# Value products of 33 groups as three float16 passes in an attention and MLP block

## The chip, the cores and the metric

One core of one Trainium2 chip runs the whole program. The metric is device time in microseconds (us), the median of the runs shown; less is better. Engines are named as the profile names them: PE is TensorE, PEld its weight loads, DVE is VectorE, ACT is ScalarE, POOL is GpSimd, SP is SyncE, which issues most of the transfers.

## The reference

Sequence 2048, width 512, 32 heads of 16 dimensions, an MLP of width 1792; all inputs and the output are float32.

```python
def _A_ref(x, wqkv, wo):
    q, k, v = ...            # (x @ wqkv), 32 heads of 16
    scores = jnp.einsum("bhqd,bhkd->bhqk", q, k) * Dh ** -0.5
    p = _softmax(scores, axis=-1)
    o = jnp.einsum("bhqk,bhkd->bhqd", p, v)
    return o.transpose(...).reshape(B, S, D) @ wo

def _B_ref(x, w1, w2):
    return silu(x @ w1) @ w2

h = x + _A_ref(_layernorm(x), A_wqkv, A_wo)
h2 = h + _B_ref(_layernorm(h), B_w1, B_w2)
```

## The kernel before

Float32 products are made from float16 parts: a number is split into a high half h and a rest l, and a product is three float16 matmuls (h·h, l·h, h·l). The one product that stays float32 is that of the softmax weights with the values.

The work of the attention is cut into 32 *items*: four heads times one of four blocks of 512 query rows; items 0 to 7 belong to the first block, 8 to 15 to the second and so on. An item has 16 chunks c of 128 keys. One item and one chunk make a *group* g = 16·i + c; there are 512. The loop over g (L1461) runs one *step* per group:

- four score matmuls (`scores`, L495), keys as weights, queries moving, 64 rows deep, so that two of different array halves run side by side. Rows 48 and 49 of a query tile hold the row's maximum, which the product so subtracts;
- four exponentials on ACT (`weigh`, L504; recorded at the helper's L113), from PSUM into a tile `pt` of 128 x 512 float32. There are 14 such buffers;
- up to four *maxima* for later items (`one_max`, L426): a 48-row matmul and a reduction on DVE (L307);
- two steps later (LAG), the *value products* of a group (`values`, L893): four float32 matmuls, one per head, with 17 columns of `va` (16 values and a one, whose product is the softmax's sum) as weights and `pt` moving. The four outputs lie at partitions 0, 32, 64 and 96 of one bank `pv`, that is, in four column tiles. The profile counts each as two matmuls, so a block has eight records;
- over 112 steps each from the fifth step of items 9, 17 and 25 on, the MLP of the query block before, as *chains*: 14 chains of 12 first products (`first_of`, L1148) and then 4 chains of 42 second products (`second_of`, L1154; three a step, so 14 steps each), cut in two halves of 64 rows and laid beside the score and maximum matmuls (`beside_products`, L1243; `half_product`, L1192). At the end of a chain of first products ACT scales the sum and SiLU is made on ACT and POOL (`bend`, L1165); at the end of a second chain (`end_second`) ACT scales (the tile `g`) and, one step later, POOL adds it to the rows `ot` and SP stores them.

After chunk 15 of an item `finish_item` (L911) copies `pv` to `pvs` on ACT, sends the sums to memory, and puts the division on an agenda at given numbers of steps after: `sums` fetches them (2), `invert` (L980) makes 1/x by four small POOL operations (6), `spread` copies the result over partitions by DMA (8), `divide` multiplies on POOL (10, odd items only).

All orders are written out: `mm`, `act`, `pool`, `dve` and `dma` pin each instruction to its place on its engine, and each engine executes in that order. Key and query tiles `ks`, `qs` form a ring of five (RING); an item's slot is i % 5. The lines of the profile are those of the helpers: L99 matmul, L106 POOL, L113 ACT, L123 DVE, L129 SP.

Of the kernel before, what the change touches and what calls it, by code (L numbers as in the profile page):

```python
# [20 lines left out]
P = 128  # L21
# [17 lines left out]
LN = 2.0 ** 10  # L39

BOUND = 23.0
PIECES = 14, 14, 4
# [5 lines left out]

LAG = 2
PTS = 14  # L50

RING = 5

HEADS = [(0, 1), (0, 0), (1, 1), (1, 0)]
# [37 lines left out]
def attention_mlp_kernel(ctx: ExitStack, tc: tile.TileContext, x, wqkv, wo, w1, w2, out):  # L92
# [100 lines left out]
    nc.gpsimd.memset(minus, -1.0)  # L193
    ones = const.tile([P, P], F32, name="ones")
    nc.gpsimd.memset(ones, 1.0)
    powers = const.tile([P, 4], F32, name="powers")
    both_s, both_w = powers[:, :2], powers[:, 2:]
    qk_s, qk_w, v_w = (powers[:, n:n + 1] for n in (0, 2, 3))
    qk_e, qk_0, v_f = (const.tile([P, 1], F32, name=name) for name in ("qk_e", "qk_0", "v_f"))

    factors = const.tile([P, 15], F32, name="factors")
    sigma, inverse = factors[:, :4], factors[:, 4:8]
    w1_s, w2_s, wo_s, o_s = (sigma[:, n:n + 1] for n in range(4))
# [47 lines left out]
    va = vpool.tile([P, KC, H, DH + 1], F32, name="va")  # L251

    def rows_of_head(t, h):
        return t[h * DH:(h + 1) * DH].rearrange("d s n -> (d s) n")

    def load_k(i, k, lo=0, n=S):
        a, j = HEADS[k]
        h = 4 * (i % 8) + 2 * a + j
        dma(ks[i % RING][64 * j:64 * j + 48, a, lo:lo + n], rows_of_head(kd, h)[:, lo:lo + n])

    def load_q(i, k):
        a, j = HEADS[k]
        h = 4 * (i % 8) + 2 * a + j
        lo = i // 8 * 512
        dma(qs[i % RING][64 * j:64 * j + 48, a, :], rows_of_head(qd, h)[:, lo:lo + 512])

# [24 lines left out]
    def maximum(i, kb, qt, a, j, n):  # L291

        piece = piece_of(i, a)
        width = 1 if i == LAST else 2
        if piece not in mx:
            mx[piece] = small.tile([P, 64], F32, name="mx", bufs=RING + 1)[:, :32 * width].rearrange(
                "p (j a q k) -> p j a q k", j=2, a=width, k=4)
            left[piece] = 32 * width
        heads = (0, 1) if j is None else (j,)
        for m, h in enumerate(heads):  # L300
            mm(space[:, n + m, :], qs[i % RING][64 * h:64 * h + 48, a, qt * P:qt * P + P],
               ks[i % RING][64 * h:64 * h + 48, a, kb * 512:kb * 512 + 512], start=True, stop=True)
        of = mx[piece][:, :, a % width, qt, kb]
        if j is None:
            pin(nc.vector.tensor_reduce(of, space[:, n:n + 2, :], axis=AX.X, op=ALU.max))  # L305
        else:
            pin(nc.vector.tensor_reduce(of[:, j:j + 1], space[:, n, :], axis=AX.X, op=ALU.max))  # L307
# [42 lines left out]
    def place_far(piece):  # L350

        i, a = piece
        n = 16 if a is None else 8
        mt = small.tile([P, P], F16, name="mt", bufs=1)
        pin(nc.sync.dma_start(mt, wide.pop(piece), transpose=True))
        split.pop(piece)

        def out():
            for j in range(2):
                rows = qs[i % RING][64 * j + 48:64 * j + 50, slice(None) if a is None else slice(a, a + 1)]  # L360
                dma(rows.rearrange("r a n -> r (a n)").rearrange("r (a b) -> r a b", b=P), mt[n * j:n * j + n, :])
            placed.add(piece)

        if at["attention"]:
            soon(1, out)
        else:
            out()

    def place_max(piece):
# [9 lines left out]
        def out():  # L379
            for j in range(2):  # L380
                dst = qs[i % RING][64 * j + 48:64 * j + 50, slice(None) if a is None else slice(a, a + 1)]
# [108 lines left out]


    def pt_tile(name):
        return bp.tile([P, 512], F32, tag="pt", name=name, bufs=PTS)

    def scores(g, k, kind="st"):  # L495

        i = g // KC
        a, j, c = head(g, k)
        assert piece_of(i, a) in placed
        ps = bank(kind)  # L500
        mm(ps, ks[i % RING][64 * j:64 * j + 64, a, c * P:(c + 1) * P], qs[i % RING][64 * j:64 * j + 64, a, :],
           start=True, stop=True)
# [39 lines left out]

    rest_sq = const.tile([P, sum(PIECES)], F32, name="rest_sq")
    norms = const.tile([P, 4], F32, name="norms")
# [24 lines left out]
    def set_factors():  # L569
# [4 lines left out]
        for to, a, f in ((h_f, inverse[:, :1], 1 / LN), (g_s, w1_s, 1 / 32.0), (g_half, w1_s, 1 / 64.0),  # L574
                         (out_f, inverse[:, :1], 32.0), (o_minus, o_s, -1.0), (o_twice, o_s, 2.0)):
            pool("tensor_scalar", to, a, f, None, op0=ALU.mult)
        pool("tensor_tensor", out_f, out_f, inverse[:, 1:2], ALU.mult)
        pool("tensor_tensor", wo_f, inverse[:, 2:3], inverse[:, 3:], ALU.mult)
# [27 lines left out]
    def measure(meanwhile):  # L606
# [58 lines left out]
    def project_v(b, t):  # L665
# [105 lines left out]
    for b in range(NB):  # L771
# [7 lines left out]
        for n, (kind, k) in enumerate(units + vs if b else units):  # L779
# [131 lines left out]
    def finish_item(i):  # L911
# [28 lines left out]
    def finish_part():  # L940
        pvs = bp.tile([P, 512], F32, name="pvs", bufs=1)
        dve("tensor_copy", pvs, pv)
        o_t = zp.tile([P, 4, P], F32, name="o_t", tag="oh")
        pool("memset", o_t, 0.0)
# [4 lines left out]
    def divide_part(part, pvs, o_t, kind="st"):  # L949
# [3 lines left out]
        halves = ps.rearrange("p t (m j r) -> p t m j r", m=2, r=32)[:, :, :, :, :DH + 1]  # L953
        both = gp.tile([P, 4, 2, DH + 1], F32, name="both", bufs=1)
# [4 lines left out]
        dve("tensor_scalar", rc, rc, o_s, None, op0=ALU.mult)  # L959
        to = o_t[:, :, 64 + 32 * part:96 + 32 * part].rearrange("p t (j d) -> p t j d", j=2)  # L960
# [104 lines left out]
    def load_rows(b, t):  # L1065
# [3 lines left out]
        else:  # L1069
            hx[t] = ks[(LAST + 1) % RING].rearrange("p a n -> p (a n)").bitcast(F32)[:, t * D:(t + 1) * D]  # L1070
        dma(hx[t], x[n * P:(n + 1) * P, :])
# [89 lines left out]
    def end_first(f, ps):  # L1161
# [3 lines left out]
        def bend():  # L1165
            t = zp.tile([P, 512], F32, name="t", tag="oh")
            act("activation", t, z, AF.Tanh, scale=0.5)
# [262 lines left out]
    def maxima(g):  # L1430

        i, c = divmod(g, KC)
        ready = at["ready"] = min(ITEMS, i + RING - (0 if c == KC - 1 else 1)) * 64
        late_now = at["step"] in late
# [26 lines left out]
    for g in range(groups):  # L1461
# [5 lines left out]
        if (g in beside) != (g - 1 in beside):  # L1467
# [37 lines left out]
        if g == 1:  # L1505
            dve("memset", pv, 0.0)
        at["group"] = g
        n = maxima(g)
# [75 lines left out]
```

## Time and profile before

| | us |
|---|---|
| median of 3 runs | 1544.13 (1543.99 to 1544.88) |
| the profiled execution, its own time | 1544.18 |
| its span | 1542.3 |
| PE busy | 1531.9 (99%) |
| DVE busy | 1364.3 (88%) |
| ACT busy | 1240.0 (80%) |
| POOL busy | 575.1 (37%) |

The time is that of the whole execution, the span goes from the first to the last instruction; the two lie 1.9 us apart. Busy times of the engines overlap, so shares alone don't say what bounds a stage. The table of stretches gives busy times for a window of the span; the timeline gives each instruction's start and length, with the idle time ahead of it and what ended that in brackets; a count behind an x means that many records in a row. A row with `xN | a, b | c` has N instructions, a us busy in all, b ns each, and c us of idle time ahead of them.

### The profile page before, as it was taken

What the parts mean: (1) busy time and instruction counts of PE and PEld (TensorE: products, weight loads), DVE (VectorE), ACT (ScalarE), POOL (GpSimd) and SP (SyncE); (2) the same over time, 40 slices, a digit from 0 to 9 for tenths busy, and PEclk for the clock granted to TensorE, in tenths of its full rate; (3) what the DMA queues carried; (4) which work ended last, traced back from release to release, by engine and by line L of the source; (5) the groups of instructions that cost most, each with busy time, mean ns of one, the idle gap of its engine ahead of it and who ended that gap; (6) DMA issues with size and microseconds to landing.
All of it is one profiled execution on the core that took longest, in us unless ns stands there. A gap on an engine that the chain in (4) does not pass through costs nothing.

```text
span 1542.3 us, 30754 instructions
## 1 busy us (share of the span) xinstructions
PE 1531.9 (99%) x11408; PEld 494.6 (32%) x11408; DVE 1364.3 (88%) x2168; ACT 1240.0 (80%) x2410; POOL 575.1 (37%) x782
## 2 busy tenths in 40 slices
PE   9999999999999999999999999999999999999999
PEld 6433322222222333333322333333322333332354
DVE  7899999999999999999999999999999999994322
ACT  5555699999987899888888998888878889888632
POOL 6643453544544444411144444301153444212100
PEclk9999999999999999999999999999999999999999
DMA  6667423333434122245424112444433221335332
GB/s 220 167 170 237 135 80 93 119 96 109 111 89 103 35 63 63 82 147 152 144 64 103 43 46 62 123 131 129 140 81 92 57 56 43 103 103 168 111 91 74
DMA packets 137058, 163.32 MB, mean 106 GB/s; under 512 B 44112, under 2 KB 81040, under 8 KB 136908
## 3 DMA queue, kind: packets, MB, share of 16 engines
q1 hardware_dynamic: 132156, 152.85, 34.6%
q10 hardware_dynamic: 4752, 8.52, 2.1%
q8 instruction: 89, 1.46, 0.4%
q14 instruction: 61, 0.50, 0.1%
HBM read 126.48 MB, written 24.63 MB: 98 GB/s over the span
## 4 chain that ended last, share of the span: by engine, by line
PE 93%; DVE 3%; ACT 2%; issue 1%; POOL 0%; DMA 0%; SPq 0%; POOLq 0%; ACTq 0%
PE ps L99 93%; ACT pt L113 1%; DVE mx L305 1%; DVE mx L307 1%; PE ps L102 1%; DMA ks<-in_A_x_dram 0%; DVE pvs L123 0%; POOL wv_l L106 0%; DVE ks L123 0%; DVE st L123 0%; ACT pvs L113 0%; ACT g L113 0%; DVE ot L123 0%; DVE xtl L123 0%; POOL rs L106 0%
## 5 line engine op out<-in xcount | busy, mean ns | idle before, releaser
L307 DVE TENSOR_REDUCE mx<-ps 128x1 f32<-128x512 f32 x1842 | 1146.1, 682 | 56.2 <-PE ps L99 12.0
L113 ACT ACTIVATE pt<-ps 128x512 f32<-128x512 f32 x2048 | 1049.7, 606 | 130.8 <-PE ps L99 128.7
L99 PE MATMUL ps<-ks,qs 48*128 48x512 f16 x2048 | 666.9, 380 | 2.6 <-DVE mx L307 1.5
L99 PE MATMUL ps<-qs,ks 64*128 64x512 f16 x2048 | 624.8, 377 | 0.6
L99 PE MATMUL ps<-pt,va 128*17 128x512 f32 x4096 | 539.1, 598 | 0.6
L99 PE MATMUL ps<-hts,w 64*128 64x512 f16 (+2 forms) x1212 | 285.0, 372 | 0.0
L99 PEld LDWEIGHTS <-ks 64*128 64x128 f16 x2048 | 174.0, 94 | 223.8 <-issue 177.6
L99 PE MATMUL ps<-w,gates 64*128 64x512 f16 (+1 forms) x938 | 230.3, 378 | 0.2 <-ACT g L113 0.2
L99 PEld LDWEIGHTS <-qs 48*128 48x128 f16 x2048 | 166.4, 94 | 67.7 <-issue 28.4
L99 PEld LDWEIGHTS <-w 64*128 64x128 f16 (+1 forms) x1212 | 101.6, 95 | 236.9 <-ACT pt L113 107.2
L106 POOL TENSOR_TENSOR ri<-rc,minus 128x16 f32<-128x16 f32 x31 | 90.6, 2924 | 208.8 <-DMA rc<-dn 208.8
L99 PEld LDWEIGHTS <-gates 64*128 64x128 f16 (+1 forms) x1082 | 88.7, 95 | 222.5 <-ACT pt L113 97.8
L99 PEld LDWEIGHTS ps<-pt,va 128*17 128x17 f32 x4096 | 68.1, 95 | 195.3 <-issue 186.6
L305 DVE TENSOR_REDUCE mx<-ps 128x2 f32<-128x1024 f32 x103 | 119.1, 1218 | 4.3 <-PE ps L99 3.5
L113 ACT ACTIVATE g<-ps,factors 128x512 f32<-128x512 f32 x80 | 54.7, 684 | 65.1 <-PE ps L99 61.0
L106 POOL TENSOR_SCALAR t<-t,factors 128x512 f32<-128x512 f32 x42 | 29.0, 691 | 184.0 <-ACT t L113 184.0
L113 ACT ACTIVATE ks<-ps 128x512 f32<-128x512 f32 x30 | 17.9, 597 | 51.9 <-PE ps L99 46.6
L106 POOL TENSOR_TENSOR ot<-ot,g 128x512 f32<-128x512 f32 x12 | 15.3, 1271 | 111.6 <-ACT g L113 111.6
L123 DVE SCALAR_TENSOR_TENSOR gh<-g,factors,gh 128x512 f16<-128x512 f32 x14 | 10.5, 752 | 52.1 <-ACT gh L113 52.1
L106 POOL TENSOR_TENSOR t<-t,g 128x512 f32<-128x512 f32 x42 | 53.7, 1279 | 3.5
L106 POOL TENSOR_TENSOR sl<-ks,sh 128x512 f16<-128x512 f32 x30 | 34.7, 1156 | 50.4 <-ACT sh L113 36.9
L106 POOL TENSOR_SCALAR nm<-nm 128x16 f32<-128x16 f32 (+1 forms) x42 | 10.8, 256 | 107.1 <-DVE nm L321 105.5
(158 smaller groups left out, 1029.7 us busy)
## 6 DMA issues: line engine op xcount, KB each, us to landing
w<-w2d SPq DMA_DIRECT2D x182, 256.0 KB
ks<-kd SPq DMA_DIRECT2D x120, 192.0 KB
w<-w1d SPq DMA_DIRECT2D x56, 256.0 KB
ks<-in_B_w_dram ACTq DMA_DIRECT2D x28, 256.0 KB
w<-in_B_w_dram SPq DMA_DIRECT2D x28, 256.0 KB
qs<-qd SPq DMA_DIRECT2D x128, 48.0 KB
kd<-sh SPq DMA_DIRECT2D x16, 256.0 KB
qd<-sh SPq DMA_DIRECT2D x16, 256.0 KB
```

The lines of the kernel that those rows point to most:

```text
L99: return tc.keep_in_program_order(nc.tensor.matmul(*a, **k))
L102: tc.keep_in_program_order(nc.tensor.transpose(*a))
L106: tc.keep_in_program_order(getattr(nc.gpsimd, op)(*a, **k))
L113: ins = getattr(nc.scalar, fn)(*a, **k)
L123: pin(getattr(nc.vector, fn)(*a, **k))
L305: pin(nc.vector.tensor_reduce(of, space[:, n:n + 2, :], axis=AX.X, op=ALU.max))
L307: pin(nc.vector.tensor_reduce(of[:, j:j + 1], space[:, n, :], axis=AX.X, op=ALU.max))
```

## The change

In 33 groups the exponentials' results are split into float16 halves, and the value products are three float16 passes in place of one float32 product. A group is one of them (`in_halves`) where its chunk is 3, 7, 11 or 15, its item is 10 to 30, and the steps from one before it to three after it lie among the second products; these are groups 207, 211, ... 255, then 335 to 383, and 463 to 487.

- ACT writes the exponential into a tile `raw` (float32, three buffers). The high half h is a cast of it, on POOL for two of the four heads (k < 2) and otherwise on ACT, except in steps with c = 2 and those that end a chain, where all are on POOL. The rest l is a subtraction on POOL. h and l lie in the two halves of the `pt` tile.
- `values` issues for such a group twelve matmuls with weights of their own: v_h·h for the four heads, then v_l·h, then v_h·l.
- The halves of the four chunks of `va` are made in item 10 by POOL (`split_chunk`) into the fifth pair of key and query tiles; from then on the ring has four slots (`slot`, `loaded`), and loads are issued one item later.
- The constant rows `fix_q` of the query tiles, zero so far, raise all exponents by a constant; `measure` computes it by three small POOL operations. The scale of the values, so far part of `v_f` and undone by `o_s`, is a constant, and the first four chunks of `va` are multiplied once more on POOL, in the projection of the third block.
- The steps of the division are 2, 7, 9, 11 in place of 2, 6, 8, 10. Buffers for maxima are four in place of six.

The core of the diff:

```diff
+START = 2
+HALVED = 3, 7, 11, 15
...
+FEWER = 2 * RING
...
-    nc.gpsimd.memset(fix_q, 0.0)
+    nc.gpsimd.memset(fix_q, 1.0)
+    raised = const.tile([16, 1], F32, name="raised")
...
+    def slot(i):
+        return i % RING if i < FEWER else (i - FEWER) % (RING - 1)
+
+    def loaded(i):
+
+        return min(ITEMS, i + RING if i < FEWER else max(FEWER + RING - 1, i + RING - 1))
...
+    def halves_of(t):
+        return t.bitcast(F16)[:, :512], t.bitcast(F16)[:, 512:]
+
+    width = H * (DH + 1)
+    spare_k, spare_q = (t.rearrange("p a n -> p (a n)") for t in (ks[RING - 1], qs[RING - 1]))
+    parts = [spare_k[:, n * width:(n + 1) * width] for n in range(7)] + [spare_q[:, :width]]
+    split_v = [(parts[n], parts[4 + n]) for n in range(4)]
...
+    def in_second(g):
+
+        return (g - marks[0]) % (8 * KC) - BEHIND - 4 * FC
+
+    def in_halves(g):
+
+        i, c = divmod(g, KC)
+        return FEWER <= i < LAST and c in HALVED and all(in_second(x) in range(START, 4 * FC) for x in (g - 1, g + 3)) and g < KC * LAST - 8
+
+    def split_chunk(n):
+
+        (h, l), v = split_v[n], va[:, HALVED[n]].rearrange("p h d -> p (h d)")
+        pool("tensor_copy", h, v)
+        low(l, v, h, "pool")
...
             pts[g, k] = pt_tile("pt")
+            if in_halves(g):
+                raw, (h, l) = zp.tile([P, 512], F32, name="raw", tag="oh", bufs=3), halves_of(pts[g, k])
+                ins = act("activation", raw, ps, AF.Exp, scale=qk_f)
+                if k < 2 or at["next"] % KC == 2 or in_second(at["next"]) % FC == FC - 1:
+                    pool("tensor_copy", h, raw)
+                else:
+                    act("copy", h, raw)
+                low(l, raw, h, "pool")
+                return ins
             return act("activation", pts[g, k], ps, AF.Exp, scale=qk_f)
...
-        dve("reciprocal", v_f, v_w)
-        pool("tensor_scalar", v_f, v_f, 1 / LN, None, op0=ALU.mult)
         dve("reciprocal", qk_e, qk_s)
         dve("scalar_tensor_tensor", qk_e, qk_e, SCALE, qk_e, op0=ALU.mult, op1=ALU.mult)
+        pool("tensor_scalar", raised, qk_s[:16], qk_s[:16], RAISE * math.log(2) / (14 * MX * SCALE), op0=ALU.mult, op1=ALU.mult)
+        pool("tensor_scalar", raised, raised, MOST, None, op0=ALU.min)
+        pool("tensor_scalar", fix_q, fix_q, raised, 1.0, op0=ALU.mult, op1=ALU.mult)
...
-        act("mul", va[:, 4 * b + t, :, 0:DH], ps.rearrange("p (h d) -> p h d", d=DH), v_f)
+        act("mul", va[:, 4 * b + t, :, 0:DH], ps.rearrange("p (h d) -> p h d", d=DH), 1 / (16.0 * LN))
...
+            if b == 2 and 2 <= n:
+                pool("tensor_scalar", va[:, n - 2, :, 0:DH], va[:, n - 2, :, 0:DH], v_s, 1.0, op0=ALU.mult, op1=ALU.mult)
...
     def values(g):
         i, c = divmod(g, KC)
         n = KC if i < LAST else HALF
+        if in_halves(g):
+            h_l, v_l = [halves_of(pts.pop((g, k))) for k in range(4)], split_v[HALVED.index(c)]
+            for m, (x, v) in enumerate(((0, 0), (0, 1), (1, 0))):
+                for k in range(4):
+                    a, j, keys = head(g, k)
+                    h = 4 * (i % 8) + 2 * a + j
+                    mm(pv[32 * k:32 * k + DH + 1, :], v_l[v][:, (DH + 1) * h:(DH + 1) * (h + 1)], h_l[k][x],
+                       start=False, stop=m == 2 and c == KC - 1)
+            if c == KC - 1:
+                finish_item(i)
+            return
...
-        steps = (1, 3, 4, 6) if u == 7 else (2, 6, 8, 10)
+        steps = (1, 3, 4, 6) if u == 7 else (2, 7, 9, 11)
         for n, fn in zip(steps, (sums, invert, spread, divide) if u % 2 else (sums, invert, spread)):
             soon(n, fn, i)
         if i == ITEMS - 2:
-            soon(10, divide_half)
-            soon(12, split_half)
+            soon(11, divide_half)
+            soon(13, split_half)
...
-        if i + RING - 1 < ITEMS and 6 <= c < 14:
-            (load_k if c % 2 else load_q)(i + RING - 1, c // 2 - 3)
+        if loaded(i) > loaded(i - 1) and 6 <= c < 14:
+            (load_k if c % 2 else load_q)(loaded(i) - 1, c // 2 - 3)
...
+        if i == FEWER and c % 3 == 2 and c < 12:
+            split_chunk(c // 3)
```

On PE the order is the same but for the blocks. This is the block of group 207, the first of the 33: before, one row for four float32 matmuls (each loads its weights by itself), between the last score matmul and the next step's second products (`gates` holds the hidden rows as weights, `w` moves).

```order
L99 LDWEIGHTS qs_107
L99 MATMUL ps<-ks_106,qs_107 128x512
L99 LDWEIGHTS ks_104
L99 MATMUL ps<-qs_105,ks_104 128x512
L99 MATMUL ps<-pt,va 17x512 x4
L99 LDWEIGHTS gates
L99 MATMUL ps<-w,gates 128x512
```

And in the changed kernel, the block's first pass and the beginning of its second; `ks4_104` and `qs4_105` are the fifth key and query tiles, which now hold halves of the values.

```order
L109 MATMUL ps_66<-qs3_103,ks3_102 128x512
L109 LDWEIGHTS ks4_104
L109 MATMUL ps_66<-pt_7871,ks4_104 17x512
L109 LDWEIGHTS ks4_104
L109 MATMUL ps_66<-pt_7907,ks4_104 17x512
L109 LDWEIGHTS ks4_104
L109 MATMUL ps_66<-pt_7879,ks4_104 17x512
L109 LDWEIGHTS ks4_104
L109 MATMUL ps_66<-pt_7915,ks4_104 17x512
L109 LDWEIGHTS qs4_105
L109 MATMUL ps_66<-pt_7871,qs4_105 17x512
```

Four matmuls have become twelve, each with a weight load of its own, at the same place. The second and third pass take the same four `pt` tiles in the same order, the third with `ks4_104` as weights again.

On ACT, around the copy of item 12's sums (`pvs`); before, exponentials alone stand on both sides of it:

```order
L113 ACTIVATE t<-g 128x512
L113 ACTIVATE pt<-ps 128x512 x20
L113 COPY pvs<-ps 128x512
L113 ACTIVATE pt<-ps 128x512 x30
L113 ACTIVATE g<-ps,factors 128x512
```

In the changed kernel, the same stretch; `raw` is written by exponentials, and a cast of it follows where it is ACT's.

```order
L123 ACTIVATE pt<-ps 128x512 x6
L123 ACTIVATE raw<-ps 128x512 x2
L123 CAST pt<-raw 128x512
L123 ACTIVATE pt<-ps 128x512 x2
L123 ACTIVATE raw<-ps 128x512 x2
L123 CAST pt<-raw 128x512
L123 ACTIVATE pt<-ps 128x512 x8
L123 COPY pvs<-ps 128x512
L123 ACTIVATE pt<-ps 128x512 x2
L123 ACTIVATE raw<-ps 128x512 x2
L123 ACTIVATE pt<-ps 128x512 x2
```

Each of the two casts ahead of the copy stands behind the last exponential of its step; group 211 behind the copy has none in its first step (c = 2), where POOL casts.

On POOL, around the division of item 12, which stands in item 13; `ri`, `rc` are the inversion, `ot<-ot,g` the add of an MLP chain, `nm` and `ns` the maxima's split. Before:

```order
L106 TENSOR_TENSOR gates<-t,gates 128x512
L106 TENSOR_TENSOR ri<-rc,minus 128x16
L106 TENSOR_TENSOR rc<-rc,ri 128x16
L106 TENSOR_SCALAR rc<-rc,factors 128x16
L106 TENSOR_TENSOR ri<-ri,rc 128x16
L106 TENSOR_TENSOR ot_1868<-ot_1868,g 128x512
L106 TENSOR_SCALAR nm<-nm 128x16
```

In the changed kernel, from group 215 (chunk 7 of item 13) to group 219 (chunk 11):

```order
L116 CAST pt<-raw 128x512
L116 TENSOR_TENSOR pt<-raw,pt 128x512 x2
L116 TENSOR_TENSOR ri<-rc,minus 128x16
L116 TENSOR_TENSOR rc<-rc,ri 128x16
L116 TENSOR_SCALAR rc<-rc,factors 128x16
L116 TENSOR_TENSOR ri<-ri,rc 128x16
L116 TENSOR_TENSOR ot_1873<-ot_1873,g 128x512
L116 CAST pt<-raw 128x512
L116 TENSOR_TENSOR pt<-raw,pt 128x512 x2
L116 CAST pt<-raw 128x512
L116 TENSOR_TENSOR pt<-raw,pt 128x512
L116 TENSOR_SCALAR nm<-nm 128x16
```

The inversion and the add now stand between the pieces of two halved groups, ahead of the second one's first cast.

More of the change, by code (lines that the diff above doesn't have):

```diff
@@ L39 @@
 LN = 2.0 ** 10
+RAISE = 14
+MOST = 2.0 ** 15
 BOUND = 23.0
@@ L193, in attention_mlp_kernel @@
     nc.gpsimd.memset(minus, -1.0)
-    ones = const.tile([P, P], F32, name="ones")
-    nc.gpsimd.memset(ones, 1.0)
     powers = const.tile([P, 4], F32, name="powers")
-    both_s, both_w = powers[:, :2], powers[:, 2:]
+    both_s, both_w, v_s = powers[:, :2], powers[:, 2:], powers[:, 1:2]
     qk_s, qk_w, v_w = (powers[:, n:n + 1] for n in (0, 2, 3))
-    qk_e, qk_0, v_f = (const.tile([P, 1], F32, name=name) for name in ("qk_e", "qk_0", "v_f"))
+    qk_e, qk_0 = (const.tile([P, 1], F32, name=name) for name in ("qk_e", "qk_0"))
     factors = const.tile([P, 15], F32, name="factors")
     sigma, inverse = factors[:, :4], factors[:, 4:8]
-    w1_s, w2_s, wo_s, o_s = (sigma[:, n:n + 1] for n in range(4))
+    w1_s, w2_s, wo_s = (sigma[:, n:n + 1] for n in range(3))
     h_f, g_s, out_f, wo_f, o_minus, o_twice, g_half = (factors[:, n:n + 1] for n in range(8, 15))
     fix_q = const.tile([16, 512], F16, name="fix_q")
-    nc.gpsimd.memset(fix_q, 0.0)
+    nc.gpsimd.memset(fix_q, 1.0)
+    raised = const.tile([16, 1], F32, name="raised")
     fix_k = const.tile([16, 512], F16, name="fix_k")
@@ L258, in load_k @@
         h = 4 * (i % 8) + 2 * a + j
-        dma(ks[i % RING][64 * j:64 * j + 48, a, lo:lo + n], rows_of_head(kd, h)[:, lo:lo + n])
+        dma(ks[slot(i)][64 * j:64 * j + 48, a, lo:lo + n], rows_of_head(kd, h)[:, lo:lo + n])
     def load_q(i, k):
@@ L264, in load_q @@
         lo = i // 8 * 512
-        dma(qs[i % RING][64 * j:64 * j + 48, a, :], rows_of_head(qd, h)[:, lo:lo + 512])
+        dma(qs[slot(i)][64 * j:64 * j + 48, a, :], rows_of_head(qd, h)[:, lo:lo + 512])
     def fixed_rows(i):
@@ L295, in maximum @@
         if piece not in mx:
-            mx[piece] = small.tile([P, 64], F32, name="mx", bufs=RING + 1)[:, :32 * width].rearrange(
+            mx[piece] = small.tile([P, 64], F32, name="mx", bufs=RING - 1)[:, :32 * width].rearrange(
                 "p (j a q k) -> p j a q k", j=2, a=width, k=4)
@@ L300, in maximum @@
         for m, h in enumerate(heads):
-            mm(space[:, n + m, :], qs[i % RING][64 * h:64 * h + 48, a, qt * P:qt * P + P],
-               ks[i % RING][64 * h:64 * h + 48, a, kb * 512:kb * 512 + 512], start=True, stop=True)
+            mm(space[:, n + m, :], qs[slot(i)][64 * h:64 * h + 48, a, qt * P:qt * P + P],
+               ks[slot(i)][64 * h:64 * h + 48, a, kb * 512:kb * 512 + 512], start=True, stop=True)
         of = mx[piece][:, :, a % width, qt, kb]
@@ L359, in out @@
             for j in range(2):
-                rows = qs[i % RING][64 * j + 48:64 * j + 50, slice(None) if a is None else slice(a, a + 1)]
+                rows = qs[slot(i)][64 * j + 48:64 * j + 50, slice(None) if a is None else slice(a, a + 1)]
                 dma(rows.rearrange("r a n -> r (a n)").rearrange("r (a b) -> r a b", b=P), mt[n * j:n * j + n, :])
@@ L380, in out @@
             for j in range(2):
-                dst = qs[i % RING][64 * j + 48:64 * j + 50, slice(None) if a is None else slice(a, a + 1)]
+                dst = qs[slot(i)][64 * j + 48:64 * j + 50, slice(None) if a is None else slice(a, a + 1)]
                 dst = dst.rearrange("r a n -> r (a n)").rearrange("r (a b) -> r a b", b=P)
@@ L541, in attention_mlp_kernel @@
     sq = small.tile([P, 3], F32, name="sq", bufs=1)
-    rest_sq = const.tile([P, sum(PIECES)], F32, name="rest_sq")
+    rest_sq = wp.tile([P, sum(PIECES)], F32, name="rest_sq")
+    ones = wp.tile([P, P], F32, name="ones")
+    nc.gpsimd.memset(ones, 1.0)
     norms = const.tile([P, 4], F32, name="norms")
@@ L574, in set_factors @@
         for to, a, f in ((h_f, inverse[:, :1], 1 / LN), (g_s, w1_s, 1 / 32.0), (g_half, w1_s, 1 / 64.0),
-                         (out_f, inverse[:, :1], 32.0), (o_minus, o_s, -1.0), (o_twice, o_s, 2.0)):
+                         (out_f, inverse[:, :1], 32.0)):
             pool("tensor_scalar", to, a, f, None, op0=ALU.mult)
+        pool("memset", o_minus, -1.0)
+        pool("memset", o_twice, 2.0)
         pool("tensor_tensor", out_f, out_f, inverse[:, 1:2], ALU.mult)
@@ L942, in finish_part @@
         dve("tensor_copy", pvs, pv)
-        o_t = zp.tile([P, 4, P], F32, name="o_t", tag="oh")
+        o_t = zp.tile([P, 4, P], F32, name="o_t", tag="oh", bufs=3)
         pool("memset", o_t, 0.0)
@@ L953, in divide_part @@
         halves = ps.rearrange("p t (m j r) -> p t m j r", m=2, r=32)[:, :, :, :, :DH + 1]
-        both = gp.tile([P, 4, 2, DH + 1], F32, name="both", bufs=1)
+        both = zp.tile([P, 512], F32, name="both", tag="oh", bufs=3)[:, :8 * (DH + 1)].rearrange("p (t j d) -> p t j d", t=4, j=2)
         rc = small.tile([P, 4, 2], F32, name="rl", bufs=1)
@@ L1069, in load_rows @@
         else:
-            hx[t] = ks[(LAST + 1) % RING].rearrange("p a n -> p (a n)").bitcast(F32)[:, t * D:(t + 1) * D]
+            hx[t] = ks[slot(LAST + 1)].rearrange("p a n -> p (a n)").bitcast(F32)[:, t * D:(t + 1) * D]
         dma(hx[t], x[n * P:(n + 1) * P, :])
@@ L1165, in bend @@
         def bend():
-            t = zp.tile([P, 512], F32, name="t", tag="oh")
+            t = zp.tile([P, 512], F32, name="t", tag="oh", bufs=3)
             act("activation", t, z, AF.Tanh, scale=0.5)
@@ L1432, in maxima @@
         i, c = divmod(g, KC)
-        ready = at["ready"] = min(ITEMS, i + RING - (0 if c == KC - 1 else 1)) * 64
+        ready = at["ready"] = loaded(i if c == KC - 1 else i - 1) * 64
         late_now = at["step"] in late
```

3 lines of the change are left out of this document (1 added, 2 removed).

## The prediction

> **What bounds the kernel now.** The page comes first: the span, the busy engines and the chain that ended last.
>
> ```profile
> span 1542.3 us, 30754 instructions
> PE 1531.9 (99%) x11408; PEld 494.6 (32%) x11408; DVE 1364.3 (88%) x2168; ACT 1240.0 (80%) x2410; POOL 575.1 (37%) x782
> PE 93%; DVE 3%; ACT 2%; issue 1%; POOL 0%; DMA 0%; SPq 0%; POOLq 0%; ACTq 0%
> L99 PE MATMUL ps<-pt,va 128*17 128x512 f32 x4096 | 539.1, 598 | 0.6
> ```
>
> TensorE holds 93% of the chain, so a shorter stream of matmuls is worth its time wherever no other engine ends later. The stage that matters is the one with second products. The sums by stretch show it beside the stretch of first products before it (us, then PE, PEld, DVE, ACT and POOL busy, granted clock, DMA share, GB/s).
>
> ```profile
> 495.22:641.55 146.33, 146.33 (x1234) 47.42 (x1232) 139.46 (x229) 132.06 (x257) 68.11 (x82) 1.00 0.24 64
> 644.17:777.42 133.25, 133.25 (x1125) 43.13 (x1123) 126.98 (x208) 109.37 (x212) 19.58 (x27) 1.00 0.43 131
> ```
>
> The second row spans 51 steps: 133.25/51 = 2.61 us each. PE is never idle, the granted clock is full. DVE works 126.98/51 = 2.49 us a step, so it has 0.12 to spare; ACT 2.14; POOL 0.38. First products leave POOL much less room (68.11 of 146.33). One step in the timeline of PE (start, length) tells what a value block costs:
>
> ```profile
> 689.58 0.39 PE L99 MATMUL ps<-w,gates 64*128 64x512 f16 x1
> 689.80 0.38 PE L99 MATMUL ps<-w,gates 64*128 64x512 f16 x1
> 690.02 0.38 PE L99 MATMUL ps<-w,gates 64*128 64x512 f16 x1
> 690.88 0.38 PE L99 MATMUL ps<-ks,qs 48*128 48x512 f16 x1
> 690.90 0.37 PE L99 MATMUL ps<-qs,ks 64*128 64x512 f16 x1
> 691.20 0.13 PEld L99 LDWEIGHTS ps<-pt,va 128*17 128x17 f32 x8 [0.33 <-issue]
> 691.20 1.05 PE L99 MATMUL ps<-pt,va 128*17 128x512 f32 x8
> 692.19 0.39 PE L99 MATMUL ps<-w,gates 64*128 64x512 f16 x1
> ```
>
> The block begins at 691.20 and the next step at 692.19: 0.985 us with the third digit. The step runs from 689.58 to 692.19. A f16 matmul of 512 columns follows the last every 0.215. The four products, eight records, take 1.05 together where one has 0.598 (the page's row above), so the column tiles run side by side; their eight weight loads are done in 0.13, at the block's start.
>
> **The new block.** 33 blocks become 12 f16 matmuls each, three passes of four column tiles. The trace has no f16 matmul with 17 columns, so its price is built from the f16 pitch and from what a change of tiling costs:
>
> ```profile
> 792.62 0.38 PE L99 MATMUL ps<-wo_l,gates 128*128 128x512 f16 x1
> 792.83 0.59 PE L99 MATMUL ps<-wo_h,gates 128*128 128x512 f16 x2
> 793.26 0.38 PE L99 MATMUL ps<-wo_l,gates 128*128 128x512 f16 x1
> 793.57 0.61 PE L99 MATMUL ps<-ks,qs 48*128 48x512 f16 x4
> 792.09 1.06 PEld L99 LDWEIGHTS <-gates 128*128 128x128 f16 x6 [0.43 <-issue]
> ```
>
> With all 128 rows the pitch is 0.21 to 0.215 too, though each matmul has a load of its own (six in the last row). The switch of tiling is 793.57 − 793.26 − 0.215 = 0.095. So: 3 × 0.215 + 0.095 + about 0.02 for the offset of four tiles = 0.76; the block saves 0.985 − 0.76 = 0.225, and 33 save **7.4 us**. Bounds: without the offset 0.74, which saves 8.1 in all; with the loads of the second and third pass in the open (0.095 each, the mean of the group below) 0.76 + 0.19 = 0.95, which saves 1.2. I take 0.76, since these very tiles hide eight loads.
>
> ```profile
> L99 PEld LDWEIGHTS ps<-pt,va 128*17 128x17 f32 x4096 | 68.1, 95 | 195.3 <-issue 186.6
> ```
>
> [...]
>
> **ScalarE.** The four exponentials keep their shape, only the tile that they write differs. Added are some 55 casts in their gaps, and the shorter steps tighten what stood there already:
>
> ```profile
> 690.25 2.06 ACT L113 ACTIVATE pt<-ps 128x512 f32<-128x512 f32 x4 [0.55 <-PE ps L99]
> 691.70 0.62 ACT L113 ACTIVATE pt<-ps 128x512 f32<-128x512 f32 x1
> 692.32 0.58 ACT L113 COPY pvs<-ps 128x512 f32<-128x512 f32 x1
> 692.84 1.10 ACT L113 ACTIVATE pt<-ps 128x512 f32<-128x512 f32 x2
> 670.31 0.68 ACT L113 ACTIVATE g<-ps,factors 128x512 f32<-128x512 f32 x1
> 670.88 2.63 ACT L113 ACTIVATE pt<-ps 128x512 f32<-128x512 f32 x5
> 73.37 0.60 ACT L113 ACTIVATE ks<-ps 128x512 f32<-128x512 f32 x1 [1.32 <-PE ps L99]
> 74.00 0.62 ACT L113 CAST sh<-ks 128x512 f16<-128x512 f32 x1
> 74.52 0.61 ACT L113 CAST xth<-xt_h 128x512 f16<-128x512 f32 x1
> ```
>
> Exponentials follow each other every (691.70 − 690.25)/3 = 0.48; a gap of 0.55 stands before the first of a step. The fourth score matmul (690.90) starts just as the first exponential ends (690.25 + 0.60), so an exponential that is late makes PE late. A cast of what ACT has just written starts 0.03 after it and lets the next start 0.52 later: 0.55 against 0.55. I take 0.2 us for all 55 (0.02 each either way: −1 to 1). After a c = 15 block comes the copy of the sums, as soon as the block has ended (692.32). With the block 0.225 shorter the copy starts at 691.70 + 0.48 = 692.18 behind the fourth exponential, the next one at 692.70, where 692.84 − 0.225 = 692.62 was due: 0.08 late, ten times, 0.8. The scaling at a chain's end takes 0.57 (670.31 to 670.88) out of 2.61 − 4 × 0.48 = 0.68, so 0.11 is left; where the step is 0.225 shorter it is 0.12 late. Two such steps (items 15 and 23) cost 0.24; three more fall together with the next part's delays.
>
> **GpSimd.** Each group adds one or two casts at a step of its own and four subtractions, and here is what they queue with:
>
> ```profile
> L106 POOL TENSOR_TENSOR gates<-t,gates 128x512 f16<-128x512 f32 x42 | 48.6, 1158 | 3.4
> L106 POOL CAST gates<-t 128x512 f16<-128x512 f32 x42 | 25.6, 610 | 2.7
> L106 POOL TENSOR_TENSOR ot<-ot,g 128x512 f32<-128x512 f32 x12 | 15.3, 1271 | 111.6 <-ACT g L113 111.6
> 700.01 2.92 POOL L106 TENSOR_TENSOR ri<-rc,minus 128x16 f32<-128x16 f32 x1 [21.93 <-DMA rc<-dn]
> 703.78 0.22 POOL L106 TENSOR_TENSOR ri<-ri,rc 128x16 f32<-128x16 f32 x1
> ```
>
> Per group 2 × 0.61 + 4 × 1.16 = 5.9 us in four steps of 2.61: enough room in the mean. But `raw` has three buffers. Count from the start of the step before the group: k0 is exponentiated third (ends at 2.25), k2 fourth, k1 and k3 one step on, and k3, due at 4.73, takes k0's buffer, which POOL must have read. Undisturbed, POOL casts from 2.35 to 2.96, subtracts until 4.19: ready at 4.29, slack 0.44. It then finishes k2 at 5.3, k1's cast and two more subtractions at 8.2. In items 13, 21 and 29 the order puts two things between c = 7's pieces and c = 11's: the inversion (703.78 + 0.22 − 700.01 = 4.0) until 12.15 and the MLP's add (1.27) until 13.4. The next k0, written at 10.44 + 2.25 − 0.225 = 12.46, waits until 13.4, is subtracted by 15.25, and the k3 due at 10.44 + 4.73 − 0.225 = 14.94 comes 0.3 late: 3 × 0.3 = 0.9. In items 14 and 22 c = 7 ends a chain, so k3's cast lies on POOL as well, 0.68 with its gap: 0.3 + 0.68 = 1.0, twice, 2.0. Together **2.9 us**. Bounds: 0, if the inversion finds an earlier gap, and 5, if each of the five is late by 1.0.
>
> **VectorE.** It loses no work of weight. Its slack is what decides:
>
> ```profile
> 690.03 0.69 DVE L307 TENSOR_REDUCE mx<-ps 128x1 f32<-128x512 f32 x1
> ```
>
> The step's last maximum (690.88) takes a bank that this reduction leaves at 690.72: 0.16, less some 0.06 for the signal, 0.10. A step of 2.385 with 2.49 of reductions leaves DVE 0.105 behind, which the three ordinary steps after it (0.12 each) make good. I take 0; if all of it shows, 33 × 0.1 = 3.3.
>
> **The rest.** The four splits of value chunks (4 × 1.8 us of POOL in item 10, beside first products whose POOL work is 68.11 of 146.33) and block 0's multiplication before attention find idle POOL and no waiting engine: 0, bounded by −0.5 to 1. Key and query loads come an item later into a ring of four; DMA is busy 0.43 in this stage: 0. One reciprocal and two small operations less: 0.1 at most.
>
> **The sum** against the profiled run's own 1544.18 (the median is 1544.13, the same): 1544.18 − 7.4 + 0.2 + 0.8 + 0.24 + 2.9 = **1540.9 us**, 3.3 less. What counts as a difference here is 0.2%, 3.1 us, so the forecast stands just beyond that line.
>
> **Rivals.**
> *POOL is never late.* If the five delays don't show, 1540.9 − 2.9 = 1538.0, and with the block at 0.74 it is 1537.3. For: the delays rest on sums of a few tenths over ten microseconds. Against: the four operations of the inversion stand in POOL's order, and it cannot pass them. Chance 0.18.
> *Weight loads in the open.* The block takes 0.95 and saves 1.2 in all; then the copies and scalings are in time, POOL's five cost about 2, casts 0.2: 1545.2. [...] The rows above speak against it; for it, no f16 load of 17 columns is in the trace. Chance 0.10.
> *VectorE's slack is gone* (0.10 isn't enough): 1540.9 + 3.3 = 1544.2, no change. For: 2.49 of 2.61 is little room. Chance 0.10.
> *The other side: four f16 tiles don't run four at a time.* Their moving tiles pass in half the time of the f32 ones (0.215 against (0.985 − 0.095)/2 = 0.445 for each of the two records of a tile). If only two run together, a pass takes 0.43, the block 1.38, 33 × 0.4 = 13 more, and with 2 of delays 1559. It decides from a pass of (0.985 − 0.115)/3 = 0.29 on. For: nothing of that kind in the trace. Against: half the bytes in each row, and full-array matmuls at 0.215. Chance 0.07.
> *POOL is late in every group.* If its operations took 1.4 times as long beside the new traffic, k3 would be 0.3 late in all 33: +10, some 1551. The rows of 610 and 1158 ns hold both under first products and elsewhere. Chance 0.05.
>
> **How the numbers follow.** The forecast, 1539 to 1543, has 0.50; the five rivals the rest. Faster by over 0.2% (below 1541.0): somewhat over half of the forecast and all of the first rival, 0.46. Slower (above 1547.2): the last two and a little of the open loads, 0.15. Between: 0.39. The range goes from 1536.5 (8.1 saved, POOL in time, casts 0.8 cheaper) to 1546.5, which holds the open loads and VectorE's loss and leaves out the last two.
>
> **What would show it.** Value blocks of about 0.76 in the groups with `ks`-named weights, four starts within 0.03; VectorE's idle before reductions unchanged; waits of an exponential into `raw` for POOL in items 13, 14, 21, 22 and 29 and nowhere else, about 0.3 and 1.0. Wrong would be: passes more than 0.29 apart, or PE waiting for exponentials in most halved groups.

## The result and the profile after

The changed kernel takes 1555.04 us (median of 5 runs, 1551.19 to 1557.82) against 1544.13: a ratio of 1.0071, with a 95% interval of 1.0059 to 1.0083. It is slower by 10.9 us where 3.3 us less was forecast, and its runs spread over 6.6 us where those of before spread over 1.0. The page of the profiled run:

```profile
span 1553.2 us, 31313 instructions
PE 1532.6 (99%) x11540; PEld 497.2 (32%) x11540; DVE 1363.2 (88%) x2165; ACT 1267.0 (82%) x2465; POOL 781.6 (50%) x1005
...
PE 90%; DVE 4%; DMA 3%; ACT 2%; issue 1%; POOL 1%; SPq 0%; POOLq 0%; ACTq 0%
PE ps L109 89%; ACT pt L123 1%; DMA mt<-ns 1%; DVE mx L321 1%; DVE mx L323 1%; DMA qs<-mt 0%; SPq L139 0%; PE ps L112 0%; DMA va<-in_A_wqkv_dram 0%; DMA w<-w2d 0%; DMA ks<-in_A_x_dram 0%; DVE st L133 0%; DVE pvs L133 0%; DVE xtl L133 0%; POOL rs L116 0%
```

New in the chain are transfers, 3%: `mt<-ns` and `qs<-mt`, which bring the maxima into the query tiles, and the weights `w<-w2d` of the second products. The waits of PE name the two that it stands still for:

```profile
PE ps L109 <- DMA qs<-mt: 5.9, 4, 3.2
PE ps L109 <- DMA w<-w2d: 3.7, 2, 1.9
```

In the kernel before neither is among PE's waits. The blocks themselves did what was forecast. This is the timeline of group 207's:

```profile
649.39 0.37 PE L109 MATMUL ps<-qs,ks 64*128 64x512 f16 x1
649.70 0.39 PE L109 MATMUL ps<-pt,ks 128*17 128x512 f16 x4
649.92 0.39 PE L109 MATMUL ps<-pt,qs 128*17 128x512 f16 x4
650.13 0.39 PE L109 MATMUL ps<-pt,ks 128*17 128x512 f16 x4
650.46 0.39 PE L109 MATMUL ps<-w,gates 64*128 64x512 f16 x1
649.71 0.10 PEld L109 LDWEIGHTS <-qs 128*17 128x17 f16 x4
649.92 0.10 PEld L109 LDWEIGHTS <-ks 128*17 128x17 f16 x4
```

Four tiles run together in each pass, passes start 0.215 apart, the loads of a pass are done under the pass before it, and the block takes 650.46 − 649.70 = 0.76 us.

Setting the start of each value block beside that of the same block before, a block of the 33 gains 0.23 us, some 0.17 where a copy of the sums follows (10), and some 0.11 where a chain's scaling stands (5). Two blocks are exceptions: group 351, with a copy behind it, gains 0.23, and group 487 only 0.06. All 33 together gain 6.2 us. Against that stand six jumps: 2.1 us at the start of item 14, 3.5 in steps 12 and 13 of that item, 0.9 at the start of item 16; then 5.1, 3.6 and 0.9 at the same places of the next query block. These are 16.1 us; the rest of the difference, about 1, is spread over steps of under 0.4.

What stands behind them is in SyncE's queue. Before, item 14 (start, length; a gap is a wait of the queue):

```profile
699.22 1.97 SPq L129 DMA_DIRECT2D w<-w2d  x2
704.03 0.32 SPq L129 DMA_DIRECT2D dr<-ri  x1
704.40 0.42 SPq L129 DMA_DIRECT2D ks<-kd  x1
708.95 0.34 SPq L129 DMA_DIRECT2D out_dram<-ot  x1
709.34 0.42 SPq L129 DMA_DIRECT2D qs<-qd  x1
709.85 0.85 SPq L129 DMA_DIRECT2D w<-w2d  x2
```

The same place in the changed kernel, which is 1.6 us later there:

```profile
700.99 2.04 SPq L139 DMA_DIRECT2D w<-w2d  x2
703.08 0.42 SPq L139 DMA_DIRECT2D ks<-kd  x1
717.35 0.32 SPq L139 DMA_DIRECT2D dr<-ri  x1
718.58 0.34 SPq L139 DMA_DIRECT2D out_dram<-ot  x1
718.97 0.42 SPq L139 DMA_DIRECT2D qs<-qd  x1
719.48 0.85 SPq L139 DMA_DIRECT2D w<-w2d  x2
```

SyncE stands from 703.5 to 717.35 before the store of the inverse, and the weights that were issued from 709.85 on before wait behind it. POOL shows why the inverse is late:

```profile
711.53 0.61 POOL L116 CAST pt<-raw 128x512 f16<-128x512 f32 x1
712.22 1.15 POOL L116 TENSOR_TENSOR pt<-raw,pt 128x512 f16<-128x512 f32 x1
713.33 2.92 POOL L116 TENSOR_TENSOR ri<-rc,minus 128x16 f32<-128x16 f32 x1
...
717.10 0.22 POOL L116 TENSOR_TENSOR ri<-ri,rc 128x16 f32<-128x16 f32 x1
717.28 1.27 POOL L116 TENSOR_TENSOR ot<-ot,g 128x512 f32<-128x512 f32 x1
718.49 0.62 POOL L116 CAST pt<-raw 128x512 f16<-128x512 f32 x1
```

Before, POOL began the inversion at 700.01, as soon as the sums had landed. Now it stands behind the pieces of chunk 7, which can't be made before their exponentials, and begins at 713.33. The weights issued at 719.48 land at 722.27 by the chain, and PE has waited 1.8 us. In item 13 the inverse is stored at 672.89, 9.4 us later than before, and the queue catches up by issuing everything at once (from there to 680.92 no gap is over 0.10). The chain from there on (start, length, what):

```profile
680.75 0.09 SPq L139
...
680.92 5.45 DMA mt<-ns
...
686.39 0.70 SPq L139
...
687.14 1.75 DMA qs<-mt
...
688.93 4.07 PE ps L109 x33
```

Before, the transpose `mt<-ns` was issued at 678.12 and the next transfer that needs it at 680.44, 2.3 us later; now 5.45 us lie between. Four weight loads were issued in the 3 us ahead of it (677.99 to 680.83), where before there were two. That is likely why: in the first experiment below, the transposes of items 14 and 22, with four loads ahead of them, took 4.7 and 4.9 us, and those of items 13 and 15, with none, 2.3. But no run changes the loads alone. PE waits for the maxima of item 14 until 688.93.

### The profile page after: what moved, and what is told of

Its sections match the earlier page's. It is cut to its first block, busy times and chain, and to the rows that moved or that the text cites. A ratio compares the mean times of both kernels' runs of the same rounds, so it can differ in the third digit from the quotient of the medians.

```text
span 1553.2 us, 31313 instructions
## 1 busy us (share of the span) xinstructions
PE 1532.6 (99%) x11540; PEld 497.2 (32%) x11540; DVE 1363.2 (88%) x2165; ACT 1267.0 (82%) x2465; POOL 781.6 (50%) x1005
## 4 chain that ended last, share of the span: by engine, by line
PE 90%; DVE 4%; DMA 3%; ACT 2%; issue 1%; POOL 1%; SPq 0%; POOLq 0%; ACTq 0%
PE ps L109 89%; ACT pt L123 1%; DMA mt<-ns 1%; DVE mx L321 1%; DVE mx L323 1%; DMA qs<-mt 0%; SPq L139 0%; PE ps L112 0%; DMA va<-in_A_wqkv_dram 0%; DMA w<-w2d 0%; DMA ks<-in_A_x_dram 0%; DVE st L133 0%; DVE pvs L133 0%; DVE xtl L133 0%; POOL rs L116 0%
## 5 line engine op out<-in xcount | busy, mean ns | idle before, releaser
L123 ACT ACTIVATE pt<-ps 128x512 f32<-128x512 f32 x1916 | 984.8, 607 | 110.0 <-PE ps L109 108.0
L109 PE MATMUL ps<-pt,va 128*17 128x512 f32 x3832 | 506.9, 601 | 0.6
L109 PEld LDWEIGHTS <-ks 64*128 64x128 f16 (+1 forms) x2404 | 181.1, 94 | 244.2 <-issue 193.2
L109 PEld LDWEIGHTS <-qs 48*128 48x128 f16 (+1 forms) x2088 | 167.6, 94 | 67.9 <-issue 28.2
L116 POOL TENSOR_TENSOR pt<-raw,pt 128x512 f16<-128x512 f32 x132 | 151.1, 1160 | 6.2
L109 PEld LDWEIGHTS ps<-pt,va 128*17 128x17 f32 x3832 | 63.8, 95 | 187.5 <-issue 178.7
L116 POOL CAST pt<-raw 128x512 f16<-128x512 f32 x77 | 47.1, 612 | 92.2 <-ACT raw L123 92.2
L123 ACT ACTIVATE raw<-ps 128x512 f32<-128x512 f32 x132 | 73.0, 615 | 2.3 <-POOL pt L116 2.1
```

The lines of the kernel that those rows point to most:

```text
L109: return tc.keep_in_program_order(nc.tensor.matmul(*a, **k))
L116: tc.keep_in_program_order(getattr(nc.gpsimd, op)(*a, **k))
L123: ins = getattr(nc.scalar, fn)(*a, **k)
```

## The experiments

**Theory:** SyncE's queue is held by its stores of late results of POOL, and what stands behind them, weights and maxima, comes late. **Rivals:** POOL's lateness acts directly, by exponentials that wait for a `raw` buffer, or by too much work in these items; or the blocks cost something. Each kernel was timed in five rounds beside the kernel before (the last in three); the kernel before was at 1543.95 to 1544.08.

**The inversion earlier.**

```diff
+        early = any(in_halves(KC * (i + 1) + c) for c in HALVED)
-        steps = (1, 3, 4, 6) if u == 7 else (2, 7, 9, 11)
+        steps = (1, 3, 4, 6) if u == 7 else (2, 5 if early else 7, 9, 11)
```

> The inversion is put on the agenda 5 steps after an item's end in place of 7 wherever the next item has halved groups; it then stands on GpSimd between the pieces of chunk 3 and those of chunk 7. Theory (SyncE's queue is held by the store of the inverse, so weight loads and the maxima's transpose leave late): the waits of TensorE for qs<-mt and w<-w2d go, some 16 us, and 1538 to 1541 us is left of 1555. Rival (GpSimd has too much work in these items, whatever the order): the same pieces, the same waits, 1551 or more.

Measured: 1541.43 us, ratio 0.9987 (0.9978 to 0.9996), 0.4 above what the theory expected. The waits for `qs<-mt` and `w<-w2d` are gone from PE's list, with the pieces unchanged. In item 14 the store of the inverse now leaves at 704.9. So the place of four small operations decided on 13.6 us. The order changed for POOL and SyncE alike, so this alone doesn't separate the theory from the first rival. Two jumps are left, 1.1 and 1.7 us, where the inversion and an add of the MLP now stand ahead of the pieces of chunk 7 in items 15 and 23.

**The pieces without their use.**

```diff
-                raw, (h, l) = zp.tile([P, 512], F32, name="raw", tag="oh", bufs=3), halves_of(pts[g, k])
+                raw, (h, l) = pts[g, k], halves_of(zp.tile([P, 512], F32, name="parts", tag="oh", bufs=3))
...
-        if in_halves(g):
+        if False:
```

> All pieces are made as in the changed kernel, by the same engines in the same order, but into tiles that nobody reads, and the value products stay float32 as before; the exponentials write pt directly, so none waits for a raw buffer. Theory (SyncE held by the late inverse): the stalls come without the gain, about 1544 + 16 = 1558 to 1563 us. Rival (exponentials that wait for raw buffers make the loss): these waits can't be, so 1544 to 1546 us.

Measured: 1555.92 us, ratio 1.0076 (1.0063 to 1.0089): 12.0 us more, two less than the least expected. The waits of PE:

```profile
PE ps L109 <- DMA qs<-mt: 4.9, 6, 1.4
PE ps L109 <- DMA w<-w2d: 4.0, 3, 1.6
```

The same two transfers, and no exponential that waits for POOL; casts of ACT wait for it in two places, 0.7 us together. So the loss doesn't need the raw buffers, nor the blocks.

**The blocks without the pieces.**

```diff
-                raw, (h, l) = zp.tile([P, 512], F32, name="raw", tag="oh", bufs=3), halves_of(pts[g, k])
...
+                return act("activation", halves_of(pts[g, k])[0], ps, AF.Exp, scale=qk_f)
...
-                       v_l[v][:, ...], h_l[k][x],
+                       v_l[v][:, ...], h_l[k][0],
```

> The float16 blocks without the pieces: the exponential writes the high half directly, nothing is cast or subtracted, and the third pass multiplies the high half again, so the low half of the softmax weights is left out. Theory: 33 blocks of 0.76 us, no late inverse, 1544.1 - 7.0 = 1537 us, within 1. Rival (the blocks themselves cost, by a lower clock or by waits of VectorE): 1540 or more.

Measured: 1538.07 us, ratio 0.9961 (0.9948 to 0.9974): 5.9 us less, 1.1 short of what was expected. The five steps with a chain's scaling gain 0.10 each, 0.6 less in all than at 0.23, group 487 gains 0.05, and a step of item 31, far from any block, loses 0.26. The others gain 0.23 and 0.17 as in the changed kernel, and no wait of PE is new. Beyond that the blocks cost nothing.

**Both stores from POOL's own queue.**

```diff
-        dma(dr[i].rearrange("k (a b) -> (k a) b", b=16), rc)
+        pin(nc.gpsimd.dma_start(dr[i].rearrange("k (a b) -> (k a) b", b=16), rc))
...
-            dma(out[n * P:(n + 1) * P, :], h)
+            pin(nc.gpsimd.dma_start(out[n * P:(n + 1) * P, :], h))
```

> GpSimd's order of operations is left as in the changed kernel; only the store of the inverse and that of the finished output rows are issued from GpSimd's own queue, so SyncE no longer waits for GpSimd there. Theory (SyncE held): weight loads and the transpose leave in time, 1539 to 1543 us, with the exponentials' waits for raw buffers of about 1 us in items 14 and 22 left over. Rival (GpSimd's lateness as such): 1552 or more.

Measured: 1558.59 us, ratio 1.0090 (1.0077 to 1.0104). By the number, the rival, 15.6 us over the most that the theory allowed. But the cause of the loss has changed. PE's and ACT's waits in this kernel:

```profile
PE ps L109 <- ACT raw L123: 5.9, 5, 1.8
PE ps L109 <- ACT pt L123: 3.8, 5, 0.8
PE ps L109 <- DMA qs<-mt: 0.7, 1, 0.7
ACT raw L123 <- POOL pt L116: 11.8, 5, 3.0
```

The wait for weights is gone and that for maxima is down to 0.7, as the theory has it. In their place exponentials wait 11.8 us for raw buffers, 2.1 in the changed kernel, since issuing the stores takes POOL's time:

```profile
718.37 0.22 POOL L116 TENSOR_TENSOR ri<-ri,rc 128x16 f32<-128x16 f32 x1
718.88 0.64 POOL L1053 DMA_DIRECT2D dr<-ri  x1 [0.29 <-POOL ri L116]
719.55 1.28 POOL L116 TENSOR_TENSOR ot<-ot,g 128x512 f32<-128x512 f32 x1
721.13 0.56 POOL L1247 DMA_DIRECT2D out_dram<-ot  x1 [0.30 <-POOL ot L116]
721.69 0.62 POOL L116 CAST pt<-raw 128x512 f16<-128x512 f32 x1
```

That is 0.29 + 0.64 + 0.30 + 0.56 = 1.8 us more between the inversion and the next cast. Nor was SyncE quite free: the fetch of the stored inverse, `den<-dr`, waits in its queue for the store to land, in item 14 from 709.78 to 720.69. The experiment changed more than one thing, and its time settles nothing; the next one leaves POOL's operations alone.

**The same results, stored later.** POOL's operations stand as in the changed kernel, save the division's multiplication; SyncE's stores stand further back.

```diff
-        dma(dr[i].rearrange("k (a b) -> (k a) b", b=16), rc)
+        def issue():
+            dma(dr[i].rearrange("k (a b) -> (k a) b", b=16), rc)
+
+        if i % 8 < 7 and i < ITEMS - 3 and any(in_halves(KC * (i + 1) + c) for c in HALVED):
+            soon(4, issue)
+        else:
+            issue()
...
-        steps = (1, 3, 4, 6) if u == 7 else (2, 7, 9, 11)
+        late_issue = any(in_halves(KC * (i + 1) + c) for c in HALVED) and i < ITEMS - 3
+        steps = (1, 3, 4, 6) if u == 7 else (2, 7, 13 if late_issue else 9, 15 if late_issue else 11)
...
-            dma(out[n * P:(n + 1) * P, :], h)
+            soon(4, dma, out[n * P:(n + 1) * P, :], h)
```

> GpSimd makes the inverse at the same place of its order as in the changed kernel, but SyncE issues its store 4 steps later (the spreading and the division move along), and the store of finished rows 4 steps later as well, so that SyncE reaches them when GpSimd is done. Theory (SyncE's queue held): no wait for w<-w2d and none for qs<-mt, 1540 to 1544 us with about 1 us each left for the raw buffers in items 14 and 22 and what the clock adds. Rival (the late work of GpSimd is the loss, whoever waits for it): 1550 or more.

Measured: 1542.46 us, ratio 0.9988 (0.9979 to 0.9997), inside what the theory expected. In item 14:

```profile
707.68 4.18 SPq L139 DMA_DIRECT2D w<-w2d  x2
711.91 0.42 SPq L139 DMA_DIRECT2D ks<-kd  x1
715.94 0.32 SPq L139 DMA_DIRECT2D dr<-ri  x1
717.17 0.34 SPq L139 DMA_DIRECT2D out_dram<-ot  x1
```

The inverse is stored at the same point of the item as in the changed kernel (counted from value block to value block, half way from that of step 10 to that of step 11 in both, and just behind that of step 10 in items 13 and 15), yet the weights have gone out ahead of it. 12.6 us come back with POOL as late as ever. This separates the theory from its rivals. What POOL's lateness costs directly is left: ACT waits 2.1 us for raw buffers in two places, and items 14 and 22 lose 1.15 us each. The wait for maxima isn't quite gone, though it was expected to be: PE's list has 0.5 us, and 0.9 and 0.4 lost at the starts of items 14 and 22.

**The division's steps alone,** in the kernel before.

```diff
-        steps = (1, 3, 4, 6) if u == 7 else (2, 6, 8, 10)
+        steps = (1, 3, 4, 6) if u == 7 else (2, 7, 9, 11)
...
-            soon(10, divide_half)
-            soon(12, split_half)
+            soon(11, divide_half)
+            soon(13, split_half)
```

> The kernel before with nothing but the division's steps of the change (2, 7, 9, 11 in place of 2, 6, 8, 10). Theory: GpSimd is idle there and takes the inversion as soon as the sums land, so only the place in SyncE's queue moves: 1544 us, within 1. Rival (the step by itself is too late): 1548 or more, with waits for qs<-mt.

Measured: 1543.54 us, ratio 0.9997 (0.9988 to 1.0006), no difference. One step later does nothing by itself, where POOL is free.

**The add moved as well,** with the inversion at 5.

```diff
-        soon(1, store)
+        soon(3 if t == 2 else 1, store)
```

> The inversion 5 steps after the item's end as in the run before, and the add of the third second-product chain 3 steps after the chain's end in place of 1, so that it stands behind the pieces of chunk 7 in items 15 and 23. Theory: the two waits for raw buffers left there (1.1 and 1.7 us with the clock) go, 1541.4 - 2.7 = 1538.7 us, within 0.7. Rival (the inversion alone holds these pieces up): 1541 or more.

Measured: 1539.21 us, ratio 0.9969 (0.9958 to 0.9980), the fastest version of the change: 4.9 us under the kernel before, 15.8 under the changed one, 1.1 above the blocks alone. The jump in item 15 is gone, that in item 23 is 0.6.

**A late inverse alone,** in the kernel before.

```diff
-        pool("tensor_tensor", rc, x, minus, ALU.pow)
+        for _ in range(5 if i in (12, 13, 14, 20, 21, 22, 28) else 1):
+            pool("tensor_tensor", rc, x, minus, ALU.pow)
```

> The kernel before, with the first operation of the inversion made five times over in the items 13, 14, 15, 21, 22, 23 and 29 (results the same), so that the inverse and the add behind it come some 12 us later on a GpSimd that has nothing else to do there; no piece, no raw buffer, no float16 block. Theory (SyncE's queue held by the two stores): TensorE waits for qs<-mt and w<-w2d again, 1544 + 8 to 14 = 1552 to 1558 us. Rival (the pieces, or the new blocks, are needed for the loss): 1544 to 1546 us.

Measured: 1579.12 us, ratio 1.0223 (1.0206 to 1.0240). The direction is the theory's, with no pieces and no new blocks; the size is two and a half times the most that was expected. The waits of PE:

```profile
PE ps L99 <- DMA w<-w2d: 23.5, 8, 5.2
PE ps L99 <- DMA qs<-mt: 1.7, 2, 1.4
```

I had taken the changed kernel's loss as the measure. But the waits alone are 25.2 us here. The inverse is later: in item 15 its store leaves at 771.28, when PE has already stood still for 0.5 us for the weights behind it, where in the changed kernel it leaves just behind the value block of step 10 and those weights hold up nothing. And it stands one step further forward in SyncE's queue, so that more of the weights wait behind it. Which of the two makes more of the waits was not tried. The clock adds to them (the profiled run's mean is 0.991): four times after a wait it stands at 0.50 for 6.83 us (from 679.11, 774.69, 1085.30 and 1133.09), with 20.8 us of PE's work in these stretches, so about 10 us more.

## Why the prediction was wrong

- **The new block** was right: 0.76 us, 0.23 saved where 0.225 was forecast, loads hidden: four loads of 17 columns are done from 649.71 on, within 0.10 us, beside the pass that began at 649.70. The rivals of open loads and of tiles that run two by two fall.
- **ScalarE** was right: 0.17 in place of 0.23 where a copy follows, 0.06 lost against 0.08 forecast; 0.10 in place of 0.23 at a chain's scaling in the run of the blocks alone, 0.13 lost against 0.12. By the prediction's terms the blocks alone gain 7.4 − 0.8 − 5 × 0.12 = 6.0; they gained 5.9.
- **VectorE** was right: the blocks alone gain what PE and ACT leave, so its slack of 0.10 was enough.
- **GpSimd** was right in what it counted: waits for raw buffers of 1.1 us in items 14 and 22, forecast 1.0. Of the three delays of 0.3 in items 13, 21 and 29 none shows as a wait; a step of about 0.1 is all that the starts show there. The rival of a POOL late in every group falls. With SyncE out of the way (the run with later stores) 2.3 us is what the lateness costs in those two items, against 2.9 for all five.
- **The step that failed** is "The rest": "Key and query loads come an item later into a ring of four; DMA is busy 0.43 in this stage: 0." It looked at the transfers' traffic, not at the queue that issues them. The GpSimd part put the end of the inversion at 12.15 us after the start of the step ahead of chunk 7, which is some 9 us later than before, and followed that to the next cast alone. The result of the inversion is also stored, by SyncE, and SyncE waits for it with weights and maxima behind. It's a term of 16 us that the sum had at nothing: 9.6 of it are PE's waits for these two, and some 5 the lower clock after three of them (the last section). No rival held it: all of them were of PE, ACT, DVE or POOL, and neither of the two signs of being wrong that were named came up. The row that would have shown it is `dr<-ri` at 704.03, 0.03 after POOL's last operation of the inversion: SyncE was already waiting for it in the kernel before.

The forecast, which is the sum without that term, is 1540.9; the run in which SyncE is free gives 1542.46, of which 1.3 us are what the maxima still lose. So the terms that were counted had the right mechanism and nearly the right sizes, and the queue that was left out turned a small gain into a loss.

## What to carry to other kernels

When work is put ahead of an operation on an off-path engine, follow that operation's result to the queue that sends it, and ask what stands behind it there: a store that waits holds every later load of its queue, though the bytes have all the room (SyncE stood for 13.8 us in item 14, and in its last stretch, 716 to 719.5, the DMA engines were busy 0.05). Before, look for queues that already wait for the operation; one that issues its store 0.03 us after the result has no slack. The remedy is a place in an order: either the small operation goes ahead of the new work (1541.4, and 1539.2 with the add moved as well), or the store goes further back in its queue (1542.5).

## What the runs showed of the hardware

A pause of TensorE can cost more than its length. In stretches of 3.41 us, the changed kernel shows (us, PE, PEld, DVE, ACT, POOL, granted clock, DMA share, GB/s):

```profile
685.11:688.52 3.41, 2.12 (x17) 0.42 (x14) 2.54 (x5) 2.24 (x5) 3.33 (x5) 1.00 0.03 6
719.24:722.65 3.41, 1.62 (x18) 0.53 (x12) 2.20 (x5) 1.79 (x4) 3.33 (x4) 1.00 0.86 273
722.65:726.06 3.41, 3.41 (x18) 0.47 (x14) 1.38 (x2) 1.68 (x3) 2.96 (x6) 0.50 0.77 242
726.06:729.47 3.41, 3.41 (x38) 1.43 (x36) 3.15 (x6) 2.65 (x6) 0.67 (x1) 1.00 0.94 249
1036.67:1040.08 3.41, 3.41 (x17) 0.75 (x18) 1.87 (x3) 1.55 (x4) 0.00 (x0) 0.50 0.55 198
1070.81:1074.22 3.41, 3.41 (x18) 0.59 (x16) 1.71 (x3) 1.37 (x4) 3.05 (x6) 0.50 0.81 219
```

After the wait of 1.8 us for weights in item 14 the clock was 0.50 for 3.41 us, which adds about as much again: 3.5 us were lost there. It fell so after three of the waits, each time with PE busy throughout, so it cost some 3 × 1.7 = 5 us of the 16. The starts of the three stretches at 0.50 lie 314.02 and 34.14 us apart, 92 times 3.413 and 10 times 3.414; in the last experiment the four lie 95.58, 310.61 and 47.79 apart, 28, 91 and 14 times as much. So in each of the two runs the falls lie whole multiples of one length apart, that of the changed kernel's stretches at 0.50 (3.41), whenever the waits came. The wait of 1.7 for maxima in item 14 ends at 688.93, and a mark ten such lengths ahead of the first fall (an estimate: 722.65 − 10 × 3.413 = 688.52) cuts it in two; PE was busy for 2.12 us of the 3.41 up to that mark and for 3.00 of the 3.41 behind it, and the clock stayed at 1.00. So where a pause lies between such marks seems to matter beside its length; no run moves a pause alone. How much idle time it takes isn't settled: PE was busy for 1.62 us of the stretch ahead of the first fall, and in the last experiment a stretch of the same length with 1.63 (723.49 to 726.90) was followed by none: from 725 to 729 PE was busy for 0.90 of 4.00 us, and the clock was 1.00 there and in the 4.00 us after.

The clock doesn't explain all of the spread of 6.6 us between the changed kernel's runs: the fastest, 1551.19, has a mean granted clock of 1.000, but those at 1557.28 and 1557.82 have 0.997 and that at 1555.04 has 0.996. The cause of the spread stays open.
